# Sliding-window attention with a soft mixture of experts: fp32 scores taken once, two heads side by side, and exponentials transposed on TensorE

## The chip, the core and the metric

The kernel runs on one core of a Trainium2 chip. Five engines work side by side: TensorE (PE; PEld is its weight load), VectorE (DVE), ScalarE (ACT), GpSimd (POOL) and SyncE (SP), which here issues the DMA transfers. Operands lie in SBUF, 128 partitions wide. TensorE writes PSUM, eight banks of 2 KB a partition. The metric is the device time of one execution in microseconds (us).

## What is computed

Attention over 4 batches x 8 heads, 576 positions, 64 wide, with a linear position bias and a causal window of 128; then a soft mixture of 8 experts with 4 slots each; then a two-layer network.

```python
scores = (q @ k.T) / 8                         # (4, 8, 576, 576)
scores = where((rel >= 0) & (rel < 128), scores - slopes * abs(rel), -1e9)   # rel = query - key, slopes = 2**-(h+1)
attn = exp(scores - max(scores)); attn /= sum(attn) + 1e-9
x = (attn @ v)                                 # as (2304, 512)
logits = x @ phi                               # 32 slots
d = softmax of logits over the tokens; slot_input = d.T @ x
slot_out[e] = relu(slot_input[e] @ w1[e]) @ w2[e]
y = softmax of logits over the slots @ slot_out
out = leaky_relu(y @ w_in) @ w_out
```

## The kernel before

The whole program is one stream of units in an order set by numbers. Each unit (a few instructions on one engine) has an offset in a table, `XO` for the 32 heads and `YO` for the router work of the four batches; a head g's unit is due at g plus its offset, the units are sorted by that, and each engine runs its instructions in this order. SyncE's loads are put into the same order: `issue` sends what is due, and between that a few pieces of expert weights (256 KB each, paced by the head's number, as long as there is free SBUF).

For one head the attention goes so:

- Q and K are loaded with two positions in a row of 512 bytes (`load_qk`), and turned by six transposes (L266) into PSUM.
- ScalarE writes the rounded parts `kb`, `qb` (L279, fp32r, the format with which one pass per product is enough), VectorE the rests into `kq` (L284, L286), GpSimd the copies of the rounded parts beside the rests (L292).
- The scores are taken twice. Once with queries on partitions and the rounded parts alone (`smax`, L306): VectorE adds the mask and takes the row maximum (L316). The maxima are transposed (L325), copied (L330) and sent by a DMA (L333) into a row of `qb`, so that the second scores carry them along. Rows of constants in `kb` and `qb` carry the position bias.
- The second time with keys on partitions (`scores`, L351 and L352: rests and rounded parts), 1088 columns in two PSUM tiles. ScalarE takes the exponential of 512 columns at a time (L359), GpSimd sets what lies outside the window to zero (L367 to L377).
- Since keys are on partitions, the exponentials are at once the weights of the products with V (`attend`, L416, 16 products of 65 columns on the two column halves of the array; the 65th column gives the sum).
- VectorE normalizes (L431, L433, L437) into `xs`.

The router work for a batch (`batch_parts`) lies between the heads: transposes of x (L460, L471), logits (L482), maxima over the tokens, slot inputs (L606, L612). Then come the expert products (L839, L891), bound up with the loading of the expert weights, and the network (L1015), 200 us long, with the weights decoded on the way. In the trace, an fp32 product of the program is two instructions (32 for `attend` of a head); a transpose is one.

PSUM in the attention stage: one tile of products with V, `TPB` = 3 tiles "tp" for turns, two "sm" for the first scores, two "st" for the second.

Of the kernel before, what the change touches and what calls it, by code (L numbers as in the profile page):

```python
# [9 lines left out]
F32 = mybir.dt.float32  # L10
F32R = mybir.dt.float32r
# [6 lines left out]
MROW = 96  # L18


@with_exitstack
def attn_softmoe_ffn(ctx: ExitStack, tc: tile.TileContext, q, k, v, phi, w1, w2, w_in, w_out, cst_in, out):
# [12 lines left out]
    TPB = 3  # L35
    R = 3
# [3 lines left out]
    WN = [5, 1, 0, 2, 3, 0, 0]  # L40
    XO = {"Z": -0.1, "TK": -3.1165, "HK": -2.9597, "DK": -2.2105, "LK": -2.68, "TQ": -3.2042, "HQ": -3.0925,
# [4 lines left out]
    YO = {"xt0": 4.4699, "xt0c": 4.6501, "xt1": 5.7337, "xt1c": 5.7794, "xr": 5.5092, "xrc": 5.6877,  # L46
          "lg": 6.5781, "lga": 6.9084, "xt2": 7.4832, "xt2c": 7.6846, "xt3": 9.7716, "xt3c": 9.8712,
          "xs": 9.4718, "xsc": 9.7691, "lh": 10.0639, "lgc": 10.0708, "pm": 10.6372, "lx": 10.7576,
          "bm": 11.6027, "bmv": 11.8446, "ln": 10.8721, "lnc": 10.9955, "bmx": 12.1976, "dxv": 12.0436,
          "dxa": 12.5969, "bt": 12.663, "btv": 12.7744, "bta": 12.9593, "sl": 12.8123, "slv": 13.1223,  # L50
          "ds": 13.3756, "dsv": 13.7379, "tm2": 12.6955, "tme": 13.0753, "cb": 13.9763, "tm3": 12.7455,
          "cb2": 13.9963, "cb3": 14.0163, "cb4": 14.0363}
    ZA = {"DQK": 0.8, "DV": 1.62, "DVS": 1, "W0": -2.2, "EARLY": 0.8, "L0": 3.0, "L1": 4.0,
# [22 lines left out]
    VW = 5 * VH * (D + 1)  # L76
    VP = -(-VW // 16) * 16
    XG = 5 * 4 * D
    sizes = [("nat", 1536), ("ex", 1536 + VP), ("vt1", VP), ("x2", XG), ("vt2", VP), ("vt0", VP), ("pt", 1536), ("x0", XG), ("x1", XG),
# [40 lines left out]
    with tc.manual_schedule():  # L120
# [7 lines left out]
        fctx, cctx = ExitStack(), ExitStack()  # L128
        fr = fctx.enter_context(tc.tile_pool(name="fr", bufs=1, side="right"))
        kb, qb, kq = [], [], []  # L130
        for i in range(R):
            kb.append(fr.tile([128, S], F32R, name=f"kb{i}"))
            qb.append(fr.tile([128, 640], F32R, name=f"qb{i}"))
            kq.append(fr.tile([128, 2 * S + 64], F32R, name=f"kq{i}"))
# [1017 lines left out]
```

## Time and profile before

| What | us |
|---|---|
| Runs of the kernel: median of 3 (lowest to highest) | 435.62 (435.59 to 436.35) |
| Profiled execution: span from first to last instruction | 434.6 |
| TensorE busy / VectorE / ScalarE / GpSimd | 419.8 / 284.1 / 239.0 / 140.5 |
| Attention stage, about | 0 to 165 |
| Expert products, about | 173 to 205 |
| Two-layer network | 205 to 434 |

Of the profiled execution the page gives the span; the times of the runs stand beside it, the median 1.0 us above. How to read it: busy time on TensorE is an upper view, since its products overlap and their ends are modelled; how often instructions start says more. A stage has its own limit, so shares are read by stage. "Idle before" with a name behind an arrow tells who ended a wait.

### The profile page before, as it was taken

The numbers are of one execution on the slowest core, as the hardware profiler recorded it, in microseconds if no ns is written. First come the engines' busy times: TensorE is split into PE (matmuls) and PEld (weight loads), VectorE is DVE, ScalarE is ACT, GpSimd is POOL, SyncE is SP. The second block draws the span as 40 slices with busy tenths as digits, with TensorE's granted clock in tenths as the row PEclk, the third lists the DMA queues.
The fourth block names the chain that finished last, engine by engine and source line by source line (L and its number), as shares of the span: only waits on it lengthen the run. The fifth ranks groups of instructions, "written<-read, shape, count | busy, mean of one in ns | idle before, by whom it ended". The sixth has DMA issues, their size and how long they took to land.

```text
span 434.6 us, 9853 instructions
## 1 busy us (share of the span) xinstructions
PE 419.8 (97%) x3480; PEld 338.2 (78%) x3480; DVE 284.1 (65%) x894; ACT 239.0 (55%) x555; POOL 140.5 (32%) x331
## 2 busy tenths in 40 slices
PE   7898999999999999999999999999999999999996
PEld 6797889888788886333877888788878888888885
DVE  7898899999999964112999885767552233225242
ACT  4586777677678733021886765555554344344440
POOL 6497788687778845020000002020202000000000
PEclk9999999999999999999999999999999999999999
DMA  7768777778867979999987005000000003004012
GB/s 163 222 185 230 227 221 215 219 207 243 229 197 220 261 254 391 321 407 413 411 305 245 31 2 193 2 1 0 2 0 0 2 9 137 0 0 148 0 74 72
DMA packets 66801, 70.15 MB, mean 161 GB/s; under 512 B 23168, under 2 KB 42016, under 8 KB 66752
## 3 DMA queue, kind: packets, MB, share of 16 engines
q1 hardware_dynamic: 66304, 69.24, 49.5%
q8 instruction: 28, 0.46, 0.4%
q10 hardware_dynamic: 448, 0.28, 0.2%
q14 instruction: 21, 0.17, 0.1%
HBM read 64.70 MB, written 4.72 MB: 160 GB/s over the span
## 4 chain that ended last, share of the span: by engine, by line
PE 84%; DVE 6%; DMA 5%; issue 2%; POOL 1%; ACT 1%; DVEq 0%; SPq 0%; POOLq 0%; ACTq 0%
PE acc L1015 45%; PE o_ps L416 6%; PE ph L992 4%; PE sm L306 4%; PE pb L839 3%; PE pb L891 3%; PE st L352 3%; PE st L351 3%; PE tp L266 3%; DMA qb<-ms 2%; DMA ar<-in_q_dram 2%; DVE kq L284 1%; DMA ar<-in_k_dram 1%; PE tp L460 1%; PE tp L482 1%
## 5 line engine op out<-in xcount | busy, mean ns | idle before, releaser
L1015 PE MATMUL acc<-p,p 128*128 128x512 f32 x648 | 158.7, 390 | 0.0
L1015 PEld LDWEIGHTS acc<-p,p 128*128 128x128 f32 x648 | 120.7, 188 | 24.5 <-issue 1.7
L1005 DVE TENSOR_TENSOR p<-ar,p 128x384 fp32r<-128x384 f32 x96 | 52.9, 556 | 89.6 <-ACT ar L1001 89.4
L997 ACT ACTIVATE p<-ph 128x384 fp32r<-128x384 f32 (+1 forms) x97 | 47.5, 491 | 92.4 <-PE ph L992 92.4
L316 DVE CUSTOM_DVE_ANT_0 junk<-sm,ar 128x256 bf16<-128x256 f32 (+2 forms) x160 | 53.6, 374 | 4.5 <-PE sm L306 4.1
L1015 PE MATMUL acc<-b,p 128*128 128x512 f32 x216 | 53.6, 392 | 0.0
L785 POOL TENSOR_TENSOR p<-ar,p 128x512 fp32r<-128x512 f32 x8 | 10.6, 1329 | 124.9 <-ACT p L785 108.7
L359 ACT ACTIVATE ar<-st 128x512 f32<-128x512 f32 x64 | 38.3, 599 | 17.2 <-PE st L352 9.8
L1001 ACT ACTIVATE ar<-ph 128x384 f32<-128x384 f32 x96 | 47.1, 490 | 0.0
L1015 PEld LDWEIGHTS acc<-b,p 128*128 128x128 f32 x216 | 40.1, 188 | 8.2 <-DVE ql L1030 0.4
L416 PE MATMUL o_ps<-ar 128*64 128x65 f32 x992 | 41.3, 227 | 0.0
L416 PEld LDWEIGHTS o_ps<-ar 128*64 128x64 f32 x992 | 36.5, 137 | 4.7 <-issue 1.0
L351 PE MATMUL st<-kq 128*128 128x256 f32 (+1 forms) x160 | 39.7, 277 | 0.0
L352 PE MATMUL st<-qb,kb 128*128 128x256 f32 (+1 forms) x160 | 35.7, 270 | 2.1 <-DMA qb<-ms 2.1
L306 PE MATMUL sm<-kb,qb 128*128 128x256 f32 (+2 forms) x160 | 34.6, 310 | 2.6 <-DVE mn L316 1.0
L279 ACT ACTIVATE qb<-tp 64x288 fp32r<-64x288 f32 x64 | 28.0, 437 | 14.0 <-PE tp L266 13.2
L992 PE MATMUL ph<-p,p 128*128 128x384 f32 x96 | 33.1, 350 | 0.0
L266 PE MATMUL tp<-ident,ar 96*128 96x96 f32 x192 | 28.5, 258 | 2.3 <-DMA ar<-in_q_dram 1.4
L352 PEld LDWEIGHTS st<-qb,kb 128*128 128x128 f32 (+1 forms) x160 | 28.6, 179 | 2.5 <-DMA qb<-ms 2.5
L284 DVE SCALAR_TENSOR_TENSOR kq<-tp,qb 64x288 fp32r<-64x288 f32 x64 | 29.2, 457 | 1.9
L279 ACT ACTIVATE kb<-tp 64x288 fp32r<-64x288 f32 x64 | 28.0, 437 | 4.4 <-PE tp L266 3.0
L286 DVE TENSOR_TENSOR kq<-tp,kb 64x288 fp32r<-64x288 f32 x64 | 29.1, 454 | 1.7
(204 smaller groups left out, 618.0 us busy)
## 6 DMA issues: line engine op xcount, KB each, us to landing
p<-in_moe_w_dram SPq DMA_DIRECT2D x56, 256.0 KB
p<-in_moe_w_dram SPq DMA_DIRECT2D x7, 1024.0 KB
p<-in_moe_w_in_dram SPq DMA_DIRECT2D x5, 1024.0 KB
p<-in_moe_w_out_dram SPq DMA_DIRECT2D x5, 1024.0 KB
ar<-in_q_dram SPq DMA_DIRECT2D x32, 144.0 KB
ar<-in_k_dram SPq DMA_DIRECT2D x31, 144.0 KB
out_dram<-ar SPq DMA_DIRECT2D x17, 256.0 KB
ar<-in_v_dram SPq DMA_DIRECT2D x32, 128.0 KB
```

The source lines that it names most:

```text
L266: nc.tensor.transpose(p[:, 96 * u:96 * u + 96], n[:, 128 * u:128 * u + 128], ident[0:96, 0:96])
L279: nc.scalar.activation(out=b1, in_=pr, func=AF.Copy, scale=2.0 ** (g % H - 2) if half else 1.0)
L306: nc.tensor.matmul(sl, lhsT=Q1[:, 128 * t:128 * t + mr], rhs=K1[:, c0:c1], start=True, stop=True)
L316: nc.vector.tensor_tensor_reduce(out=jk[0:mr, 0:n], in0=sl, in1=maskt[0:mr, m0:m0 + n], op0=ALU.add, op1=ALU.max, accum_out=mn[g % 2][0:mr ...
L351: nc.tensor.matmul(sl, lhsT=KX[:, k0:k1], rhs=QA[:, q0:q1], start=True, stop=False)
L352: nc.tensor.matmul(sl, lhsT=kb[g % R][:, k0:k1], rhs=qb[g % R][:, q0:q1], start=False, stop=True)
L416: nc.tensor.matmul(o_ps[64 * u:64 * u + 64, t, :], lhsT=lt, rhs=r, start=st, stop=sp, tile_position=(0, 64 * u))
L992: nc.tensor.matmul(p, lhsT=mst[:, 128 * f:128 * f + 128], rhs=rhs, start=True, stop=True)
L997: nc.scalar.activation(out=G[t0, f][0][:, c], in_=H1[t0, f][:, c], func=AF.Prelu, alpha=0.01)
L1001: nc.scalar.activation(out=gg, in_=H1.pop((t0, f)), func=AF.Prelu, alpha=0.01)
L1005: nc.vector.tensor_tensor(out=g2, in0=G0.pop((t0, f)), in1=g1.bitcast(F32), op=ALU.subtract)
L1015: nc.tensor.matmul(acc[t0][t], lhsT=(g1, g1, g2)[k][:, 128 * t:128 * t + 128], rhs=(WO1, WO2, WO1)[k][c][:, i], start=(f == f0 and k == 0) ...
```

## The change

Attention works on pairs of heads (i = 0 to 15), and the scores are taken once, in fp32, with queries on partitions.

- Q and K of two heads lie side by side in 128 columns; rows of 64 positions' tiles are loaded in pieces of 256 bytes (`load_qk`, three DMAs for each of Q and K). Positions are cut at 64, 192, 320, 448, so that the first 64 are a tile of their own.
- Eight transposes of 128x128 and two small ones turn them (`turn`, `turn_rest`); head 0 of the pair is then on partitions 0 to 63, head 1 on 64 to 127. One copy on VectorE (K) and one scaled copy on ScalarE (Q) bring them to SBUF, two small ones the rest.
- `scores`: ten fp32 products for a pair, five a head, on 64 rows of the array each, the heads in turn.
- `smax` on VectorE adds mask and position bias (now in the mask tile, loaded as a constant) and writes the sum in fp32 to SBUF beside the maximum. `bias` on GpSimd scales the maxima; `expo` on ScalarE takes the exponential with the maximum as bias, one instruction a block (five a head).
- `flip`: the exponentials are transposed on TensorE, 16 of 128x128 a pair, and copied back to SBUF (`flip_c`, three on ScalarE, one on VectorE).
- `attend`: 17 products a head as before with 64-column weights; each head of the pair has its own PSUM tile.
- Gone: rounded parts and rests, the copies, the transposed maxima and their DMA, the masks and clears on GpSimd.
- All other PSUM tiles of the stage come from one ring of six (`gt`). The tables `XO`, `YO`, `LAST` are new; the router's work is the same, its logits now in two sums for every batch.

```diff
-    XO = {"Z": -0.1, "TK": -3.1165, "HK": -2.9597, ...
+    XO = {"TK": -3.52, "EK": -3.40, "TQ": -3.42, "EQ": -3.31, "TT": -3.32, "ET": -3.2,
+          "S": -2.0, "X0": -1.9, "X1": -1.85, "Y0": -1.7, "Y1": -1.6, ...
...
+        def gt(shape=(128, 512)):
+            return ps.tile(list(shape), F32, tag="g", name="g", bufs=GB)
...
-            put(t.rearrange("p (j c) -> p j c", j=3), src.rearrange("(j p r) d -> p j (r d)", j=3, r=2), n, (half, g))
+            for a in range(2):
+                put(t[:, 0:4, a, :], src[a, 64:S, :].rearrange("(t p) d -> p t d", p=128), n, (half, i))
+            put(t[0:64, 4, :, :], src[:, 0:64, :].rearrange("h p d -> p h d"), n, (half, i))
...
+        def evac_k(i):
+            nc.vector.tensor_copy(kqs[i % R][0][:, 64:S], tps.pop((0, i)))
+
+        def evac_q(i):
+            nc.scalar.activation(out=kqs[i % R][1][:, 64:S], in_=tps.pop((1, i)), func=AF.Copy, scale=qsc[:, i % HB:i % HB + 1])
...
+        BLK = [[(4, 0, 0, 64, 0, 128), (0, 0, 64, 192, 64, 64), (1, 64, 256, 256, 192, 0)],
+               [(2, 192, 0, 256, 320, 0), (3, 320, 256, 256, 448, 0)]]
+
+        def scores(i):
+            K, Q = kqs[i % R]
+            for c in range(2):
+                for a in range(2):
+                    sts[i, a, c] = gt()
+                for t, k0, o, n, q0, m0 in BLK[c]:
+                    for a in range(2):
+                        r = slice(64 * a, 64 * a + 64)
+                        nc.tensor.matmul(sts[i, a, c][:, o:o + n], lhsT=Q[r, q0:q0 + 128], rhs=K[r, k0:k0 + n],
+                                         start=True, stop=True, tile_position=(64 * a, 0))
...
-                        out=jk[0:mr, 0:n], in0=sl, in1=maskt[0:mr, m0:m0 + n], op0=ALU.add, op1=ALU.max,
+                        out=piece(i, a, c)[:, o:o + n], in0=p[:, o:o + n], in1=maskt[:, m0:m0 + n], op0=ALU.add, op1=ALU.max,
...
+        def expo(a, c):
+            def f(i):
+                for t, k0, o, n, q0, m0 in BLK[c]:
+                    e = piece(i, a, c)[:, o:o + n]
+                    j = (t + 1) % 5
+                    nc.scalar.activation(out=e, in_=e, func=AF.Exp, scale=slope(i, a), bias=nb[i % 2][:, a, j:j + 1])
...
+        def flip(a, c):
+            def f(i):
+                pts[i, a, c] = p = gt()
+                e = piece(i, a, c)
+                for j in range(4):
+                    nc.tensor.transpose(p[:, 128 * j:128 * j + 128], e[:, 128 * j:128 * j + 128], ident)
+            return f
+
+        def flip_c(a, c):
+            def f(i):
+                cp = nc.vector.tensor_copy if (a, c) == (0, 1) else nc.scalar.copy
+                cp(out=ptl[2 * a + c], in_=pts.pop((i, a, c)))
```

TensorE in the middle of the stage, before: one head with no router work between (L266 turns, L306 first scores, L351 and L352 second scores, L416 products with V, L325 the transpose of the maxima).

```order
L266 MATMUL tp<-ident,ar 128x96 x3
L306 MATMUL sm<-kb_88,qb_89 128x256 x2
L266 MATMUL tp<-ident,ar 128x96 x3
L416 MATMUL o_ps<-ar 64x65 x16
L325 MATMUL tp<-ident,mn_99 5x128
L306 MATMUL sm<-kb_91,qb_92 64x192
L306 MATMUL sm<-kb_91,qb_92 128x128
L306 MATMUL sm<-kb_91,qb_92 128x256
L351 MATMUL st<-kq_96 128x256
L352 MATMUL st<-qb_95,kb_94 128x256
```

Now, one pair of heads from its second transpose of exponentials on (L331 these transposes of the exponentials, L292 scores, L259 and L265 turns, L354 products with V):

```order
L331 MATMUL g<-ident,ss_90 128x128 x4
L331 MATMUL g<-ident,ss_91 128x128 x4
L331 MATMUL g<-ident,ss_92 128x128 x4
L292 MATMUL g<-kqt 128x64 x2
L292 MATMUL g<-kqt 128x192 x2
L292 MATMUL g<-kqt 128x256 x6
L259 MATMUL g<-ident,ar 128x128 x8
L265 MATMUL g<-ident,ar 128x64 x2
L354 MATMUL o_ps_106<-ar,pt_93 64x65 x9
L354 MATMUL o_ps_106<-ar,pt_94 64x65 x8
L354 MATMUL o_ps_107<-ar,pt_95 64x65 x9
L354 MATMUL o_ps_107<-ar,pt_96 64x65 x8
```

Where a head had its second scores and the products with V with nothing between exponential and product, a pair now has the four transposes of the exponentials (the first stands ahead of these rows), then the next pair's scores, the turns of the pair behind that, and the products with V of the pair whose exponentials were transposed at the start.

VectorE at the same place, before: the rests of Q and K, then a normalization and the maxima of a later head.

```order
L284 SCALAR_TENSOR_TENSOR kq_90<-tp,qb_89 64x288 x2
L286 TENSOR_TENSOR kq_90<-tp,kb_88 64x288 x2
L431 TENSOR_SCALAR rs<-o_ps 128x5
L316 ISA junk,mn_98<-sm,ar 64x192
L316 ISA mn_98 64x1
L433 RECIPROCAL rs<-rs 128x5
L437 TENSOR_TENSOR ar<-o_ps,rs 128x5x64
L316 ISA junk,mn_98<-sm,ar 128x128
L316 ISA mn_98 128x1
L316 ISA junk,mn_98<-sm,ar 128x256
```

Now: the end of a pair's maxima, the copy of K, both normalizations, the copy of one quarter of the transposed exponentials, and the next maxima:

```order
L302 ISA ss_92,mx_99<-g,ar 128x256
L302 ISA mx_99 128x1
L270 COPY kqt<-g 128x512
L366 TENSOR_SCALAR rs<-o_ps_106 128x5
L368 RECIPROCAL rs<-rs 128x5
L373 TENSOR_TENSOR ar<-o_ps_106,rs 128x5x64
L366 TENSOR_SCALAR rs<-o_ps_107 128x5
L368 RECIPROCAL rs<-rs 128x5
L373 TENSOR_TENSOR ar<-o_ps_107,rs 128x5x64
L337 COPY pt_94<-g 128x512
```

The rests are gone; two copies of 128x512 came.

## Rows read from the trace of the kernel before

**Rows 1.** Busy time by stage: stretch, its length, each engine (instructions), clock, DMA share, GB/s.
```profile
60.00:140.00 80.00, 77.28 (x1075) 68.15 (x1074) 76.15 (x320) 58.28 (x143) 62.40 (x155) 1.00 0.77 218
...
170.00:205.00 35.00, 34.82 (x318) 12.69 (x318) 8.00 (x35) 5.63 (x18) 6.05 (x15) 1.00 1.01 381
```

**Rows 2.** VectorE in order of time, one head: start us, us, operation, count.
```profile
90.97 0.17 DVE L431 TENSOR_SCALAR rs<-o_ps 128x5 f32<-128x5 f32 x1
...
92.14 0.42 DVE L316 CUSTOM_DVE_ANT_0 junk<-sm,ar 128x256 bf16<-128x256 f32 x1
...
92.49 0.42 DVE L316 CUSTOM_DVE_ANT_0 junk<-sm,ar 128x256 bf16<-128x256 f32 x1
...
93.29 0.95 DVE L284 SCALAR_TENSOR_TENSOR kq<-tp,qb 64x288 fp32r<-64x288 f32 x2
94.27 0.94 DVE L286 TENSOR_TENSOR kq<-tp,kb 64x288 fp32r<-64x288 f32 x2
95.25 0.17 DVE L431 TENSOR_SCALAR rs<-o_ps 128x5 f32<-128x5 f32 x1
```

**Rows 3.** The chain that ended last, in order of time: start us, us, what.
```profile
9.15 3.19 DMA ar<-in_q_dram
...
22.82 1.19 PE o_ps L416 x32
...
26.41 1.37 PE o_ps L416 x32
...
212.37 2.04 PE acc L1015 x9
```

**Rows 4.** Line 437: duration min/median/max in ns, first and last start.
```profile
L437 DVE TENSOR_TENSOR ar<-o_ps,rs x31: 472/491/493, 25.5 to 164.0; 128x320 f32<-128x320 f32 x31
```

**Rows 5.** TensorE in order of time: start us, us, operation, count.
```profile
90.42 0.60 PE L460 MATMUL tp<-ident,ar 128*128 128x128 f32 x4
...
115.15 1.07 PE L612 MATMUL tp<-ar,dn 128*32 128x256 f32 x16
...
164.19 0.97 PE L416 MATMUL ol<-ar 128*64 128x65 f32 x16 [0.23 <-POOL ar L367]
...
176.21 7.07 PE L839 MATMUL pb<-p,ar 128*32 128x512 f32 x64
```

**Rows 6.** Groups by line and shape up to 190 us: busy us, mean ns, idle before.
```profile
L460 PE MATMUL tp<-ident,ar 128*128 128x128 f32 x64 | 10.2, 279 | 0.0
...
L482 PE MATMUL tp<-ar,phi_sb 128*32 128x144 f32 x128 | 6.0, 293 | 0.3 <-DVE ar L474 0.3
...
L622 DVE COPY SI<-tp 128x512 f32<-128x512 f32 x1 | 0.7, 691 | 0.0
...
L464 ACT COPY ar<-tp 128x256 f32<-128x256 f32 x2 | 0.7, 372 | 2.2 <-PE tp L460 2.2
```

**Rows 7.** The page's groups by line, and those of 173 to 205 us.
```profile
L1015 PE MATMUL acc<-p,p 128*128 128x512 f32 x648 | 158.7, 390 | 0.0
...
L839 PE MATMUL pb<-p,ar 128*32 128x512 f32 x112 | 12.6, 595 | 0.0
```

**Rows 8.** SyncE's queue in order of time.
```profile
1.75 0.42 SPq L158 DMA_DIRECT2D ar<-in_q_dram  x1
...
5.48 3.57 SPq L158 DMA_DIRECT2D ar<-in_v_dram  x6
```

**Rows 9.** Transfers from 6 to 10, 182 to 186 and 60 to 140 us.
```profile
DMA packets 2818, 0.63 MB, mean 157 GB/s; under 512 B 2818, under 2 KB 2818, under 8 KB 2818
...
q1 hardware_dynamic: 2818, 0.63, 76.6%
...
q1 hardware_dynamic: 813, 1.63, 105.1%
...
DMA packets 25559, 17.44 MB, mean 218 GB/s; under 512 B 11203, under 2 KB 20709, under 8 KB 25542
...
q1 hardware_dynamic: 25542, 17.23, 76.1%
```

More of the change, by code (lines that the diff above doesn't have):

```diff
@@ L203, in attn_softmoe_ffn @@
+        for half in (1, 0):
+            load_qk(half, 0)
+        for j in range(3):
+            o, i, _, _ = bulk.pop()
+            nc.scalar.dma_start(out=o, in_=i)
+            send()
+        nc.sync.dma_start(out=maskt, in_=cst_in[:, 0:256])
+        nc.sync.dma_start(out=qsc, in_=cst_in[:, 256:260])
         warm(WN[0])
@@ L233, in attn_softmoe_ffn @@
             load_v(i)
-        issue(0)
+        issue(1)
         pieces = []
@@ L247, in attn_softmoe_ffn @@
         nxt_piece = [0]
-        late = len(pieces) + (off["x0"] - off["vt1"]) // 512 + R * (3 * S + 704) // 512
-        for r, t in pieces[:-3]:
+        late = len(pieces) + (off["x0"] - off["vt1"]) // 512 + 13
+        for r, t in pieces[:-5]:
             queue(r, t)
@@ L312, in smax_v, with turn @@
-        def smax_v(part):
-            def f(g):
-                for t, sl, m0, n, mr in sms.pop((part, g)):
-                    jk = small.tile([128, 256], mybir.dt.bfloat16, tag="junk", name="junk", bufs=2)
+        def turn(half):
+            def f(i):
+                flush((half, i))
+                n = nat(half, i)
+                tps[half, i] = p = gt()
+                for t in range(4):
+                    nc.tensor.transpose(p[:, 128 * t:128 * t + 128], n[:, t].rearrange("p h d -> p (h d)"), ident)
+            return f
@@ new lines, in turn_rest @@
+        def turn_rest(i):
+            tps[2, i] = p = gt()
+            for half in range(2):
+                nc.tensor.transpose(p[:, 64 * half:64 * half + 64], nat(half, i)[0:64, 4].rearrange("p h d -> p (h d)"), ident[0:64, 0:64])
+                if i + 2 < NI:
+                    load_qk(half, i + 2, 2 * i + XO["TT"] + DQK)
+        def evac_k(i):
+            nc.vector.tensor_copy(kqs[i % R][0][:, 64:S], tps.pop((0, i)))
+        def evac_q(i):
+            nc.scalar.activation(out=kqs[i % R][1][:, 64:S], in_=tps.pop((1, i)), func=AF.Copy, scale=qsc[:, i % HB:i % HB + 1])
@@ L478, in f @@
                 def f():
-                    p = ts["lg"] if last and k0 else tp("lg", [128, 144], "sm")
+                    p = ts["lg"] if nm == "li" else tp("lg", [128, 144])
                     for kc in range(k0, k1):
@@ L526, in pm @@
                 m = small.tile([128, 1], F32, tag="pm", name="pm", bufs=1)
-                nc.vector.reduce_max(out=m, in_=ts["lg"] if last else L, axis=AX.X)
+                nc.vector.reduce_max(out=m, in_=L, axis=AX.X)
                 if b == 0:
@@ L657, in attn_softmoe_ffn @@
         for nm, f in UNITS.items():
[L658 to L659 removed]
+            for i in range(NI):
+                ev.append((2 * i + XO[nm], len(ev), lambda f=f, i=i: f(i)))
         for b in range(B):
```

406 lines of the change are left out of this document (141 added, 265 removed), and 8 rows, old and new, of the table XO.

## The prediction

> **What bounds the kernel now.** I read first the table by stage, then the order of time on VectorE and on TensorE, then the transfers. In the attention stage two engines look full: from 60 to 140 us TensorE is busy 77.28 of 80 us and VectorE 76.15, ScalarE 58.28, GpSimd 62.40, the DMA engines 0.77 [rows 1]. Busy time doesn't tell which of the two is the limit, so I took one head on each. On VectorE one head lasts from one L431 to the next, 90.97 to 95.25, 4.28 us, and within it the instructions stand end to end: the casts' rests (L284, L286) in pairs of 0.95 and 0.94, five maxima (L316; a 256-wide one starts 0.35 after the last), and in the 0.6 left one normalization [rows 2]. On TensorE, in the chain of waits, the first products with V of one head start at 22.82 and those of the next at 26.41, 3.59 us, with no router work and no wait between [rows 3]. The mean over the stage is (164.0 - 25.5)/30 = 4.62 us a head, from the first and last start of L437 [rows 4]. So VectorE sets the pace: the 0.34 above its 4.28 are the router's work on it. TensorE needs 32 x 3.59 = 115 us and the router's part (below, 19): 134 after 22.82, so 157, where the last L416 group starts at 164.19 and ends at 165.16 [rows 5]. It is only some 8 us behind VectorE. That is the whole point: a change that relieves VectorE gains at most until TensorE is the limit, and this change also alters what TensorE does. After the stage, 170 to 205 us, TensorE is busy 34.82 of 35 on the expert weights with the DMA engines at 1.01 [rows 1]. The granted clock is 1.00 in all these rows.
>
> **VectorE, ScalarE, GpSimd: what goes and what comes, for a pair of heads.** The casts' rests go (2 x 1.9 us), and the masks, copies and clears on GpSimd; four small bias products stay there. VectorE keeps ten maxima (64, 192 and three times 256 wide for each head; at 0.35 or less 3.5 us), keeps two normalizations (1.2), and gets two copies of 128x512 out of PSUM, which the trace has once, at 0.69 [rows 6]: 6.1, with the router's 0.7 about 6.8, where it was 9.2. The maxima now write fp32 instead of bf16; I count this at nothing, and if it cost 0.1 us each VectorE would be at 7.8. ScalarE gets ten exponentials of at most 256 columns for two of 512, at 0.37 for a 256-column copy [rows 6] at most 3.7, four passes over 128x512 at no more than VectorE's 0.69 and two small ones, 3.2: 6.9, and about 1 for the router. Both stay under what follows for TensorE, which hides them.
>
> **TensorE, for a pair.** The prices are steps from start to start, since its intervals overlap: the length of a group less one duration, over the number of steps.
> - Transposes: four in 0.60 with 0.279 each is (0.60 - 0.28)/3 = 0.107 [rows 5, 6]; I take 0.115 for the changes between groups. The exponentials are 16 of them, 1.85 us, all new. K and Q take 10 instead of 12, 1.15.
> - Scores. Gone are the rounded scores and the two-term scores with the transpose of the maxima. New are ten fp32 products, each on 64 rows, 1024 columns a head. A 512-column pass is 2.04/9 = 0.227 us on L1015 [rows 3]. An fp32 product shows in the trace as two instructions, each of 595 ns at 512 columns against the 390 of L1015, so of two passes [rows 7]: 1024 x 4 passes x 0.227/512 = 1.8 us a head. If the two heads, which stand on different halves of the array's rows and write different banks, run at the same time, that is 1.8 a pair; if one after the other, 3.6. The trace has no product on half the rows. The nearest row is L839: 64 fp32 instructions on four column quarters in 7.07 us [rows 5], 0.10 each, where one alone would need 0.45. I take the overlapped end, nearest to this row, and 0.2 for entering and leaving: 2.0. Both ends stay for the range.
> - Products with V: 34 for 32, in two runs instead of four. A head's run takes 1.19 to 1.37 [rows 3]: 2.6.
> - The router's part is kept. Four L460 groups of 0.45, two L482 groups (16 of 128, 0.75 each by their busy time), L612 with 1.07 [rows 5, 6], and by these prices some 1.5 of smaller ones: 5.8 a batch, 1.4 a pair.
>
> Sum: 1.85 + 1.15 + 2.0 + 2.6 + 1.4 = 9.0 us a pair, where the pace now is 9.24. TensorE's own work doesn't fall; it rises a little (7.6 against 7.2 without the router). What is won is the difference to VectorE's pace, and the start.
>
> The Trainium skill puts a figure on the product on half the rows, "TensorE: Matmul & The Clock Gate", Part 3: four row tiles came to 3.07 times the speed of one after the other, 77% of four. Two tiles at 77% would make 2.3 us of the 1.8, and 7 us on the whole sum; no run here shows it yet.
>
> **The start.** The third head's Q comes behind V on SP; the chain waits for this transfer from 9.15 on, for 3.19 us [rows 3]. In the changed order eleven SP loads (three for each of Q of pair 0, Q and K of pair 1, and two constants) stand ahead of V, twelve of V, the router's matrix, and then six for pair 2. At 0.45 for the first kind (0.42 for one of Q) and 0.6 for V (six in 3.57) [rows 8] that is, from 0.8 on, 5 + 7.7 + 2.6, so 16.1; with 3 us to land 19. The turns of pair 2 stand in TensorE's row ahead of the products of pair 0, so these start at about 19, two heads at once, where the first head's start at 22.82 now. From 17 to 22 is possible.
>
> **The sum.** From 19 on: 16 runs of 2.6 (41.6), 15 times the exponentials (27.8), 14 scores (28), 13 turns (15), the router less its tail (19): 131. TensorE stood idle 3.4% of the time in [rows 1], 2.72 of 80; with as much, 136. The stage ends at 155 instead of 165.2: 10 us. The tail has one addition more on VectorE, 0.3 us. Everything behind it is as before. 434.6 - 10 + 0.3 = 425 us of span; the median of the runs is 1.0 above the span, so about 426, and I say 425.5.
>
> **Transfers.** Q and K now come in rows of 256 bytes, twice as many packets. From 6 to 10 us all 2818 packets were under 512 bytes and took 76.6% of 16 engines: 17.4 ns each [rows 9]. A packet of the weights takes 1.051 x 64 / 813 = 83 ns [rows 9]. From 60 to 140 us, 76.1% of 1280 engine-us less 11203 x 17.4 and 4833 x 83 ns leaves 378 for 9506 packets of 512 bytes: 40 ns [rows 9]. So two short ones cost 35 where a long one cost 40; nothing is lost. The Trainium skill, "DMA: Bandwidth & Descriptors", Specifications, speaks against the change: line rate needs 512 bytes or more. By that rule a short packet would cost what the long one does and the stage's 0.77 would become over 1.0, which is the second rival; the row at 17.4 ns disagrees. On SP a pair issues 10 loads of Q, K and V and as many weights as before, for 7 loads and two of the maxima; at 0.45 these 14 or 15 issues take 6.5 us of 9, as now. Weights are paced by heads, so as many lie in SBUF at the stage's end.
>
> **The rivals.**
> First, slower: the two heads' score products run one after the other. Each pair then costs 1.6 to 1.8 us more on TensorE, in 14 of 16 pairs (two lie in the start): +25, so 450. It decides from 0.7 us a pair on, where the 10 us are used up; so more than half the overlap has to be there. For it: no row has a product on half the rows. Against it: the four quarters of L839, and the loops issue the two heads in turn. 0.13.
> Second, the transfers become the limit. By the rule above Q and K would cost 18432 x 40 ns / 16 = 46 us more of the DMA engines; 0.77 x 155 + 46 = 165 us, the stage would end where it does now: 434 to 437. A milder form is that the weights, at 1.01 behind the stage, come a few us late. The rows speak against the full form. 0.10.
> Third, TensorE waits in its order. From the start of a pair's scores to its last exponential lie 1.2 (first tiles), up to 3.5 of maxima, and the bias and the last two exponentials, about 1: 5.7 us; TensorE fills 5.75 ahead of the first transpose of exponentials and 7.1 ahead of the last. This fits with 1 us to spare; the six PSUM tiles that all now share could take it away. Each us a pair costs 14: 432 to 440. 0.14.
> Fourth, better than the sum: fewer waits than 3.4%, or an earlier start: 411 to 417. 0.08.
>
> **How the numbers follow.** The forecast, 417 to 431, has 0.55. The second and third rivals lie on both sides of the time before; about a third of each is within 0.2%, which is about what a measurement of this kernel can tell from no change. Faster 0.71, same 0.08, slower 0.21. The range 415 to 442 leaves out the first rival (0.13) and a little at the lower end.
>
> **What would show it.** Right: VectorE under 75% busy from 60 to 140 us and TensorE as full as now; the last normalization near 156; start-to-start of the two heads' score instructions far below their duration, a pair's scores in about 2 us; transposes at 0.11; short packets still at 17 to 18 ns. Wrong: a pair's scores in 3.6 us, TensorE waiting on ScalarE ahead of the transposes of the exponentials, the first products with V later than 22 us, or waits on DMA in the weights' stage.

## The result and the profile after

The changed kernel takes **440.57 us** (median of six runs, 439.27 to 442.10), the kernel before 435.75 (six runs beside them). The ratio is 1.010, with a 95% interval of 1.007 to 1.013: slower by about 1%. 425.5 was predicted; the time lies in the range of 415 to 442, but on the other side of the kernel before. The profiled execution has a span of 439.9 us, and its time is 441.92. All comparisons here are between undisturbed runs, except where a granted clock below 1.00 is named with the row.

The same two stretches as in [rows 1], with the same columns:

```profile
60.00:140.00 80.00, 76.06 (x1100) 64.02 (x1097) 56.92 (x272) 56.46 (x154) 8.25 (x36) 1.00 0.87 223
170.00:205.00 35.00, 33.32 (x303) 13.75 (x303) 10.95 (x48) 6.40 (x20) 7.36 (x19) 1.00 0.87 325
```

VectorE fell from 76.15 to 56.92 us and GpSimd from 62.40 to 8.25, as the change meant; TensorE is nearly as full as it was, 76.06 where it had 77.28. The relief was real, and the kernel is slower all the same.

Where the loss lies, three rows tell: the products with V and the normalization (first and last start, answering [rows 4]), and the matmuls of the last stage from the page (answering [rows 7]):

```profile
L354 PE MATMUL o_ps<-ar,pt x1088: 218/222/272, 26.9 to 169.9; 128*64 128x65 f32 x182
...
L373 DVE TENSOR_TENSOR ar<-o_ps,rs x33: 292/492/493, 28.6 to 170.8; 128x320 f32<-128x320 f32 x31, 128x128 f32<-128x128 f32 x1, 128x192 f32<-128x192 f32 x1
...
L945 PE MATMUL acc<-p,p 128*128 128x512 f32 x648 | 158.7, 390 | 0.0
```

The last product with V starts at 169.9; before it was at 164.9:

```profile
L416 PE MATMUL o_ps<-ar x992: 220/222/272, 22.8 to 163.3; 128*64 128x65 f32 x199
L416 PE MATMUL ol<-ar x32: 220/222/272, 163.2 to 164.9; 128*64 128x65 f32 x32
```

From there to the end of the span lie 439.9 - 169.9 = 270.0 us after and 434.6 - 164.9 = 269.7 before. The same 270 us, within 0.4, end every run below, so what follows needs two numbers only: the **first** product with V (the start) and the **way** from the first to the last (the steady part). Before: 22.8 and 142.1. Forecast: 19 and 136. After: 26.9 and 143.0. So 7.9 us of the miss lie in the start and 7 in the steady part.

**The start**, from the chain of waits (start us, us, what); it answers the first lines of [rows 3]:

```profile
2.19 3.48 DMA ar<-in_k_dram
...
5.80 1.09 PE g L259 x4
6.89 0.85 PE g L157 x4
...
11.00 3.93 PE g L292 x20
...
20.94 2.04 PE g L292 x20
...
26.97 1.19 PE o_ps L354 x34
```

K lands at 5.67, and then no transfer is waited for: TensorE itself is the path. Two things stand in it. L157 are filler products (two between any two pieces of the start, printed as four since an fp32 product is two instructions); those between the pieces take 25.5% of the view's 32 us, 8.2 us. And TensorE works at half speed: the first score group of 20 takes 3.93 us where the next takes 2.04, the first turn of K 1.09 where it takes 0.63 at full speed (below). This is the lower of the two levels of TensorE's clock, 1.2 GHz. A row for these us prints 1.00 only because the trace holds no record of the clock before 15.0 us, where the upper level, 2.4 GHz, begins; the durations change at the same place. TensorE had stood from 3.9 to 5.8 us, waiting for K.

**The steady part.** The row of the whole way (columns as in [rows 1]), TensorE's waits from 20 to 165 us (us in total, times, longest), and a pair in the chain that ended last, in order of time:

```profile
26.90:169.90 143.00, 134.98 (x2038) 114.84 (x2038) 96.88 (x451) 99.60 (x270) 13.73 (x60) 1.00 0.89 239
```

```profile
PE g L417 <- ACT ar L409: 5.8, 4, 1.4
PE g L292 <- ACT pt L337: 1.2, 3, 0.4
```

```profile
60.84 0.24 POOL nb L313
...
61.10 2.08 ACT ss L321 x6
63.18 0.57 ACT kqt L273
63.75 0.80 ACT ss L321 x2
...
64.86 0.80 ACT ss L321 x2
65.65 0.47 ACT ar L399
66.12 0.17 ACT ar L409
...
66.33 0.70 PE g L417 x16
67.03 1.90 PE g L331 x16
68.93 1.23 PE g L292 x12
```

TensorE is busy 135.0 of the 143.0 us and idle 8.0, where the forecast had 131 and 5. The idle part is told by the waits and the chain: bias, ten exponentials (with copies of Q between them), two copies for the router, then the router's logits (L417) and only behind them the transposes of the exponentials (L331). The logits product stands ahead of the transposes in TensorE's order and waits for a copy that stands behind all exponentials in ScalarE's. So from the first exponential to the last copy, 5.2 us, ScalarE is the chain. TensorE's own work of that time, the products with V, ends at 64.9, and it stands until 66.3.

### The profile page after: what moved, and what is told of

Its sections match the earlier page's. It is cut to its first block, busy times and chain, and to the rows that moved or that the text cites. A ratio compares the mean times of both kernels' runs of the same rounds, so it can differ in the third digit from the quotient of the medians.

```text
span 439.9 us, 9567 instructions
## 1 busy us (share of the span) xinstructions
PE 422.9 (96%) x3584; PEld 335.8 (76%) x3584; DVE 244.7 (56%) x790; ACT 238.5 (54%) x587; POOL 34.7 (8%) x103
## 4 chain that ended last, share of the span: by engine, by line
PE 86%; ACT 7%; DVE 3%; issue 1%; DMA 1%; POOL 0%; ACTq 0%; DVEq 0%; POOLq 0%
PE acc L945 45%; PE g L292 7%; PE g L331 6%; PE o_ps L354 5%; ACT ss L321 5%; PE ph L922 4%; PE pb L769 3%; PE pb L821 3%; PE g L259 2%; PE g L157 2%; PE g L417 1%; PE g L395 1%; DVE ss L302 1%; PE g L544 1%; PE ph L872 1%
## 5 line engine op out<-in xcount | busy, mean ns | idle before, releaser
L945 PEld LDWEIGHTS acc<-p,p 128*128 128x128 f32 x648 | 120.7, 188 | 24.5 <-issue 1.7
L321 ACT ACTIVATE ss<-ss,nb 128x256 f32<-128x256 f32 (+2 forms) x160 | 62.0, 456 | 30.3 <-POOL nb L313 30.3
L302 DVE CUSTOM_DVE_ANT_0 ss<-g,ar 128x256 f32<-128x256 f32 (+2 forms) x160 | 48.0, 367 | 22.2 <-PE g L292 22.1
L292 PE MATMUL g<-kqt 64*128 64x256 f32 (+2 forms) x320 | 37.0, 370 | 1.2 <-ACT pt L337 1.2
L354 PE MATMUL o_ps<-ar,pt 128*64 128x65 f32 x1088 | 37.2, 225 | 0.0
L354 PEld LDWEIGHTS o_ps<-ar,pt 128*64 128x64 f32 x1088 | 34.9, 137 | 2.1 <-issue 1.6
L337 ACT COPY pt<-g 128x512 f32<-128x512 f32 x48 | 26.1, 589 | 14.0 <-PE g L331 13.6
L292 PEld LDWEIGHTS g<-kqt 64*128 64x128 f32 x320 | 28.1, 195 | 6.1 <-issue 2.7
L331 PE MATMUL g<-ident,ss 128*128 128x128 f32 x256 | 31.4, 275 | 0.0
L331 PEld LDWEIGHTS g<-ident,ss 128*128 128x128 f32 x256 | 28.1, 141 | 1.6 <-issue 1.4
L715 DVE SCALAR_TENSOR_TENSOR ar<-ar 128x512 int32<-128x512 int32 x40 | 25.7, 686 | 0.2
L313 POOL TENSOR_SCALAR nb<-mx 128x3 f32<-128x3 f32 (+1 forms) x64 | 14.3, 224 | 130.5 <-DVE mx L302 127.0
L259 PE MATMUL g<-ident,ar 128*128 128x128 f32 x128 | 18.8, 288 | 1.9 <-DMA ar<-in_k_dram 1.9
```

The source lines that it names most:

```text
L259: nc.tensor.transpose(p[:, 128 * t:128 * t + 128], n[:, t].rearrange("p h d -> p (h d)"), ident)
L292: nc.tensor.matmul(sts[i, a, c][:, o:o + n], lhsT=Q[r, q0:q0 + 128], rhs=K[r, k0:k0 + n], start=True, stop=True, tile_position=(64 * a, 0))
L302: nc.vector.tensor_tensor_reduce(out=piece(i, a, c)[:, o:o + n], in0=p[:, o:o + n], in1=maskt[:, m0:m0 + n], op0=ALU.add, op1=ALU.max, acc ...
L321: nc.scalar.activation(out=e, in_=e, func=AF.Exp, scale=slope(i, a), bias=nb[i % 2][:, a, j:j + 1])
L331: nc.tensor.transpose(p[:, 128 * j:128 * j + 128], e[:, 128 * j:128 * j + 128], ident)
L354: nc.tensor.matmul(o[64 * u:64 * u + 64, t, :], lhsT=p[:, x:x + 64], rhs=V[:, w, a, :], start=st, stop=sp, tile_position=(0, 64 * u))
```

## The experiments

**Is the loss in the start and in the order?** Three edits of the changed kernel, one each: more warm-up products ahead of K's landing, no filler products, the logits later in TensorE's order.

```diff
-    WN = [5, 2, 0, 2, 3, 0, 0]
+    WN = [10, 2, 0, 2, 3, 0, 0]
```


> The changed kernel with ten instead of five idle products on TensorE ahead of the first transposes, which cover its wait for K from 3.9 to 5.8 us. Theory (start): after this wait TensorE works at half speed until about 15 us (first scores 4.0 us instead of 2.11, transposes 0.27 apart instead of 0.11), and every step of the start stands on that; the first products with V come at 22 to 24 us instead of 26.9 and the whole is 3 to 5 us faster, 436 to 437.5. Rival: the start waits for loads (SP issues the third pair's Q until 19.1 us), and the first products come no earlier than 26: no change beyond 1 us.

```diff
-    WN = [5, 2, 0, 2, 3, 0, 0]
+    WN = [5, 0, 0, 2, 3, 0, 0]
```


> The changed kernel without the 26 filler products that TensorE runs between the pieces of the start (13 pairs of products). Theory: they lie on the path from the landing of K at 5.7 to the first products with V; without them TensorE gets there until the transfer of the third pair's Q, which lands at 21 to 22, holds it: first products with V at 22.5 to 24 instead of 26.9, time 436 to 438. Rival: TensorE's speed falls without them and the first products come no earlier than 25: 439 to 441.

```diff
-          "lg": 5.44, "lga": 5.6, ... "lh": 9.44, "lgc": 9.55, "pm": 9.7, "lx": 9.65,
+          "lg": 5.95, "lga": 6.05, ... "lh": 9.95, "lgc": 10.05, "pm": 10.06, "lx": 10.07,
```


> The changed kernel with the router's logit products (line 417) moved from just ahead of a pair's transposes of the exponentials to just behind them, with what follows from them. Theory (waits in order): TensorE stood for some 1.4 us at these products in 4 places, for a copy that ScalarE has queued behind the exponentials, though the transposes behind it were ready; 5 to 6 us faster, about 435. Rival: the transposes wait for the same exponentials, the wait only moves to the next instruction: within 1 us of 440.6.

| kernel | first product | last | way | median us | ratio to before (95%) |
|---|---|---|---|---|---|
| changed | 26.9 | 169.9 | 143.0 | 440.57 | 1.010 (1.007 to 1.013) |
| longer warm-up | 23.7 | 167.1 | 143.4 | 439.12 | 1.0074 (1.0047 to 1.0101) |
| no fillers | 22.5 | 165.6 | 143.1 | 437.45 | 1.0043 (1.0021 to 1.0064) |
| logits later | 24.5 | 164.4 | 139.9 | 436.12 | 1.0013 (0.998 to 1.0047) |

First products and ways move as the theories said; the time of the longer warm-up, 439.12, stays above the 436 to 437.5 that was expected. The fillers cost 4.4 us of start, compared at the same half speed of the first scores (then Q of the third pair holds: its transfer ends at 20.7). With the longer warm-up the first turn takes 0.63 and the first scores 2.04, from its chain:

```profile
5.73 0.63 PE g L259 x4
...
8.59 2.04 PE g L292 x20
```

The logits are worth 3.1 us of the way; the 2.4 of start in that row belong to the start itself, which differs from one execution to the next: the trace's clock record begins at 9.7 us there and at 15.0 in the changed kernel's, so that its first scores already run at full speed. Against a start like that the longer warm-up is worth 0.8 us, against the changed kernel's 3.2. The waits with the logits later show what comes next:

```profile
PE g L259 <- DMA ar<-in_k_dram: 2.5, 3, 1.2
PE g L259 <- DMA ar<-in_q_dram: 1.9, 5, 0.5
...
PE g L417 <- ACT ar L409: 0.7, 1, 0.7
```

**What the overlap of the two heads is worth, and whether TensorE is the limit after.** The score loops in another order: inside each tile one head first, then (second edit) a whole head first; and one more transpose in each group of the exponentials.

```diff
-                for t, k0, o, n, q0, m0 in BLK[c]:
-                    for a in range(2):
+                for a in range(2):
+                    for t, k0, o, n, q0, m0 in BLK[c]:
```


> The changed kernel, with the score products of one head issued one after another and then those of the other, instead of in turn; the same products and results. If the two heads' products run at the same time in the changed kernel (20 instructions in 2.11 us), this takes the overlap away: a pair's scores should take 3.5 to 3.8 us and the time rise by 14 pairs x 1.6 = 22 us, to about 462. If the overlap does not depend on the order, or was never there, the time stays at 440.

```diff
-            for c in range(2):
-                ...
-                for t, k0, o, n, q0, m0 in BLK[c]:
-                    for a in range(2):
+            for a in range(2):
+                for c in range(2):
+                    for t, k0, o, n, q0, m0 in BLK[c]:
```


> The changed kernel with all ten fp32 score instructions of one head ahead of those of the other (before: the two heads in turn). Theory: the two heads overlap on the array only where their instructions stand next to each other; a pair's scores then take 3.2 to 3.6 us instead of 2.04, 1.2 to 1.5 more in 14 pairs, of which TensorE's waits can take up about 0.4: 451 to 457. Rival: the pace is set elsewhere than on TensorE, and the scores' length does not matter: 441 to 444.

```diff
-                for j in range(4):
+                for j in (0, 1, 2, 3, 0):
```


> The changed kernel with one transpose of each four done twice, four more 128x128 transposes a pair, 64 in all, with the same result. If TensorE is the limit through the whole stage, each costs its step of 0.11 us: 7 us slower, 447 to 448. If TensorE waits for the exponentials in each pair (a chain through VectorE, GpSimd and ScalarE sets the pace), less than half of that shows: under 444.

Measured: 441.08 (ratio 1.0101, 1.004 to 1.0162; way 144.2), 448.74 (1.028, 1.0246 to 1.0313; way 149.9), 445.23 (1.0196, 1.0135 to 1.0258; way 148.3). A pair's scores in the chains of the first and the second:

```profile
67.39 2.31 PE g L292 x19
```

```profile
71.30 3.13 PE g L293 x19
```

So with the two heads in turn 20 instructions take 2.04 us, in blocks of two or three 19 of them take 2.31, a whole head at a time 3.13: the overlap exists, and it needs neighbours in TensorE's order. (Three pairs of 14 take 2.9, in turn and in blocks alike; in turn the group waits 0.4 us in its middle there for a copy out of PSUM, the second row of TensorE's waits above.) My first expectation for the blocks, 462, was wrong because blocks of two or three still overlap; the second, 451 to 457, was too high too. By rows like that of the whole way above, TensorE's busy time rose from 135.0 to 147.4 us with a whole head at a time, and its idle time fell from 8.0 to 2.6; the difference, 6.9, is what reached the way. Of the 7 us of extra transposes 5.3 did. TensorE is the limit of the changed kernel for the larger part of the stage, and the rest is its waits.

**Was VectorE the limit before?** On this the forecast rested. Five edits of the kernel before. One rest of the casts left out on VectorE (the second scores then lack its term; zeros stand there), and both:

```diff
+            nc.gpsimd.memset(kq[i].bitcast(F32)[0:64, 0:S], 0.0)
...
-                    else:
-                        nc.vector.tensor_tensor(out=x2, in0=pr, in1=b1.bitcast(F32), op=ALU.subtract)
```


> The kernel before without one of the two rests of the casts on VectorE (the K rest, about 0.95 us a head; the second scores then lack the term with that rest). Theory: VectorE sets the pace of the attention stage before; with 3.33 + 0.34 us a head it would fall behind TensorE's 3.59 and its router work, so the stage follows TensorE and the kernel ends 5 to 8 us earlier: 428 to 431. Rival: TensorE or the transfers already set the pace, VectorE is full beside it: 434 to 436.

```diff
             def low_(g):
-                for pr, b1, x2 in pieces(g):
-                ...
+                pass
```


> The kernel before without either rest of the casts on VectorE (about 1.9 of its 4.28 us a head; the second scores then lack the terms with the rests). VectorE has nothing left that could set a pace of 4.6 us. Theory (formed after the run that left out one rest): TensorE, with the round trip of the maxima through DMA, set the pace of the attention stage before, and VectorE was only full beside it: 433 to 436. Rival, the prediction's own premise: VectorE set the pace, and the stage now follows TensorE: 426 to 430.

One transpose more per group of Q and K:

```diff
-                for u in range(3):
+                for u in (0, 1, 2, 0):
```


> The kernel before with one 96x96 transpose more in each of the 64 groups of Q and K (the first is done twice), 64 x 0.10 = 6.4 us more on TensorE, nothing on VectorE. Theory: TensorE sets the pace before, so most of it comes through: 441 to 443. Rival, the prediction's premise: TensorE has 8 us to spare behind VectorE, and 2 us or less come through: 436 to 438.

The round trip of the maxima left out, alone and with both rests; and the round trip on another queue:

```diff
         def mtr_d(g):
-            nc.sync.dma_start(out=qb[g % R][MROW:MROW + 1, :]...
+            mss.pop(g)
```


> The kernel before without the transfer that carries the rounded maxima back into the second scores (17 of it between 60 and 140 us, one a head; the second scores then lack the maxima). From the first to the last product with V lie 142.1 us in the kernel before, 142.7 without the rests, 142.7 with more transposes. Theory: this transfer, in order on SP behind the wait for the maxima, closes the loop that sets the pace; without it 135 to 138 us from the first to the last product, time 429 to 432. Rival one, VectorE after all: nothing changes as long as the rests are there: 435 to 437. Rival two, TensorE: the same 435 to 437, and the next kernel tells which.

> The kernel before without that transfer and without the rests of the casts (the second scores lack both). Theory: VectorE and the round trip are two limits of nearly the same length, each of which holds the pace when the other is taken away; without both 132 to 136 us from the first to the last product with V, time 428 to 432 (a first product as late as 27 as without the rests alone would add 4). Rival: TensorE itself sets the pace: 141 to 143 us, time 436 to 440.

```diff
-            nc.sync.dma_start(out=qb[g % R][MROW:MROW + 1, :]...
+            nc.scalar.dma_start(out=qb[g % R][MROW:MROW + 1, :]...
```


> The kernel before with the transfer of the maxima issued on ScalarE's queue, right behind the copy that makes them, instead of on SP's. If it is SP's order that makes the round trip long, the stage gets shorter by 2 to 5 us: 431 to 434. If it is the landing of the transfer itself (about 2 us), or another limit: 435 to 437; and slower, 438 to 440, if 0.7 us of issue a head on ScalarE holds its casts.

| kernel before, with | first product | last | way | median us | ratio (95%) |
|---|---|---|---|---|---|
| nothing changed | 22.8 | 164.9 | 142.1 | 435.75 | |
| one rest out | | | | 437.08 | 0.9996 (0.9964 to 1.0028) |
| both rests out | 27.3 | 170.0 | 142.7 | 439.20 | 1.0057 (1.0032 to 1.0082) |
| transposes added | 23.1 | 165.8 | 142.7 | 438.19 | 1.0022 (0.9994 to 1.005) |
| round trip out | 23.1 | 162.7 | 139.6 | 434.17 | 0.992 (0.9889 to 0.9951) |
| both rests and round trip out | 27.0 | 161.8 | 134.8 | 433.70 | 0.9898 (0.9831 to 0.9966) |
| round trip on ScalarE's queue | | | | 441.93 | 1.0098 (1.0063 to 1.0132) |

(Two rows have no way: their profiled executions had a granted clock of 0.96 from 60 to 100 us.) VectorE relieved of 1.9 us a head: the way does not move. TensorE loaded with 6.4 us: it does not move either. What does hold it then is read from TensorE's waits; first rows, in this order, of both rests out and of the round trip out:

```profile
PE st L350 <- DMA qb<-ms: 5.7, 6, 1.9
```

```profile
PE tp L325 <- DVE kq L284: 1.2, 4, 0.5
PE sm L306 <- DVE mn L316: 0.9, 2, 0.5
```

Without the rests it is the transfer of the maxima; without the transfer it is VectorE. Without both, the row from 60 to 100 us is TensorE end to end:

```profile
60.00:100.00 40.00, 39.81 (x571) 36.13 (x570) 25.63 (x133) 30.60 (x75) 33.42 (x82) 1.00 0.85 229
```

and the way is 134.8 us. So **two limits of nearly the same length** (139.6 and 142.7) stood in front of TensorE's own 134.8, each holding the pace when the other is taken away. This is shown.

Is it the transfer's landing or its issue in SP's order? On ScalarE's queue the kernel is slower by 1%, which doesn't tell them apart, since 0.70 us of issue a head then stands among ScalarE's casts. The chain without the rests does: from the start of its issue to its landing the transfer takes 4.15 us in the row below, and the issue is 0.72 of that. The landing is the larger part.

```profile
59.99 0.10 PE st L350
60.09 4.15 DMA qb<-ms
...
64.29 0.38 PE st L350
```

In the two kernels without both rests the first product comes 4 us later, which is why their times say less than their ways. This is the edit's own doing: the zeros that stand for the rests are written by VectorE at the start, from 5.4 to 9.7 us, ahead of a row of constants that the first scores need. TensorE's wait for it, without the rests:

```profile
PE sm L304 <- DVE kb L224: 4.7, 1, 4.7
```

**Does the changed kernel beat both when mended?** Four edits at once (ten warm-up products, one filler for two, logits later, and eight loads of V on ScalarE's queue):

```diff
-    WN = [5, 2, 0, 2, 3, 0, 0]
+    WN = [10, 1, 0, 2, 3, 0, 0]
...
+        for j in range(8):
+            o, i, _, _ = bulk.pop(0)
+            nc.scalar.dma_start(out=o, in_=i)
```


> The changed kernel with four things at once: ten first warm-up products instead of five, one filler product instead of two between the pieces of the start, the eight loads of V of the second and third pair on ScalarE's queue, and the logits products later in TensorE's order. Theory: the start and the waits on the logits are what the change lost; first products with V at 19 to 20.5, from there to the last ones 140 to 141 us, time 429 to 433, faster than both kernels. Rival: what the start gains comes back as waits on the transfers of Q and K later: 434 to 437.

435.05 us, ratio **0.9963** (0.9944 to 0.9982): faster than both, by 0.4% and some 1.3%, though not the 429 to 433 expected. First product at 24.7, way 137.8. The start did not get shorter: its chain runs through the V loads in ScalarE's queue. Behind them stand the load of ScalarE's function table (the 1.28 us) and the copies of Q.

```profile
4.08 4.20 DMA ar<-in_v_dram
...
8.30 0.61 ACTq L230
...
9.66 1.28 ACT L276
```

So next no filler at all, V of the third pair on SP behind its Q and K, ten warm-ups and the later logits; run twice, since its first profile had a granted clock of 0.93 from 60 to 100 us:

```diff
-    WN = [5, 2, 0, 2, 3, 0, 0]
+    WN = [10, 0, 0, 2, 3, 0, 0]
...
-        for i in range(1, NVB):
+        for i in range(1, NVB - 1):
             load_v(i)
...
+            if i == 0:
+                load_v(NVB - 1, XO["TT"] + DQK)
```


> The changed kernel with ten first warm-up products, no filler products between the pieces of the start, the loads of the third pair's Q and K ahead of those of its V on SP, and the logits products later in TensorE's order. Theory: first products with V at 19 to 20.5, as the prediction had them, and from there 139 to 141 us as in the run with four edits (24.7 to 162.5 there): 430 to 432.5. Rival: the loads that come earlier at the start are missing later, TensorE waits for Q and K, and no more than 1 us is won over the run with four edits: 434 to 435.

> The same kernel as the one with the short start (ten first warm-up products, no filler products, the third pair's Q and K ahead of its V, logits later), since the profiled execution of that one had a granted clock of 0.93 from 60 to 100 us and so cannot tell where the 4 us that the start won were lost. Theory: at a granted clock of 1.00 from the first to the last product with V lie 140 to 142 us, and the time is 433 to 434 in such an execution. Rival: SP's issue of the loads holds TensorE, 143 to 145 us at full clock too.

Ratios 0.9975 (0.9951 to 1.000) and 0.9966 (0.9932 to 1.000), medians 436.01 and 435.20: no better than the four edits, and above what was expected of either. The first product comes at 20.7 and 20.2, nearly the 19 of the forecast, but the way is 145.8 and 144.3. In the first, TensorE's clock has a part. TensorE waited for a transfer of K from 56.1 to 57.7 us, and from 58.8 to 65.6 the lower level was granted, which is worth some 3.4 us at half speed (the row of 60 to 100 us):

```profile
60.00:100.00 40.00, 39.47 (x542) 33.60 (x541) 25.50 (x120) 26.29 (x71) 3.25 (x14) 0.93 0.88 223
```

In the second the clock is 1.00 there, and TensorE waits:

```profile
PE g L259 <- ACT ss L323: 3.5, 5, 1.3
PE g L259 <- DMA ar<-in_k_dram: 2.9, 5, 0.9
PE g L259 <- DMA ar<-in_q_dram: 1.9, 6, 0.5
```

What the start wins the way gives back. Is it SP's issue of loads? All V loads on GpSimd's queue, in the kernel with the later logits, in the one with the short start, and there with the bias products on VectorE too:

```diff
-            nc.sync.dma_start(out=o, in_=i)
+            (nc.gpsimd if key[0] == "v" else nc.sync).dma_start(out=o, in_=i)
...
-                nc.gpsimd.tensor_scalar(out=nb[i % 2][:, a, r], ...
+                nc.vector.tensor_scalar(out=nb[i % 2][:, a, r], ...
```


> The changed kernel with the logits products later and all loads of V issued on GpSimd's queue instead of SP's. SP's issues fill some 71 of 80 us in the changed kernel (32 of V at 0.605, 27 of K at 0.507, 27 of Q at 0.594, 38 of weights at about 0.5). Theory: with the logits' wait gone, SP's issues hold TensorE (waits on Q and K of 4.4 us there); without V on SP the last product with V comes 3 to 5 us earlier than 164.4: 431 to 433. Rival: the landing, not the issue, is late, or TensorE's own work is the limit: 435 to 437; slower, 438 to 442, if GpSimd's issues hold the small products of the bias that ScalarE's exponentials wait for.

> The kernel with the short start, and all loads of V issued on GpSimd's queue. Theory: the short start (first products with V at 20) is then not given back, since SP keeps up: last product with V at 157 to 160, time 427 to 431. Rival: ScalarE's exponentials or the landing of Q and K hold the pace as in the run with the short start (144.3 us from first to last product): 434 to 437.

> The kernel of the run before this one (short start, all V on GpSimd's queue), with the small products of the bias on VectorE, so that no exponential waits for GpSimd any more (16 waits, 50.9 us in the run before). Theory: SP's issues were what gave the shorter start back; first products with V at 19.5 to 21, the last at 157 to 160, time 427 to 431. Rival: ScalarE's exponentials and TensorE's order hold the pace, and the last products come at 162 to 165 again: 434 to 437.

460.37, 450.82 and 444.63 us: all slower, by 1.8 to 5%. They don't answer the question, since each makes a new wait in GpSimd's order: first (of the second kernel) the exponentials for the bias, which stands behind loads that wait for their buffer, then (third kernel) the router for a product on GpSimd. Behind such waits the clock fell as well: it was at the lower level from 14.9 to 28.6 us in the second kernel, TensorE having stood from 11.7 on, and from 70.6 to 80.8 in the third, where TensorE stood from 67.1 to 75.4.

```profile
ACT ss L323 <- POOL nb L315: 50.9, 16, 14.3
```

```profile
PE g L452 <- POOL ar L447: 8.3, 1, 8.3
```

Whether SP's issues or ScalarE's exponentials hold the mended kernel **stays open**.

## Why the prediction was wrong

**The prices on TensorE held for a pair, the sum did not.** Per pair: transposes of the exponentials 1.90 (1.85 said), scores 2.04 to 2.11 (2.0), turns 1.02 + 0.27 (1.15), products with V 2.24 (2.6). Together 7.5 where 7.6 was said, and the first rival fell. The Trainium skill has 3.07 times for four row tiles ("TensorE: Matmul & The Clock Gate", Part 3); an estimate from that, 77% for two tiles, would have made the scores 2.3 us; the 2.04 here are 88% of the ideal 1.8. But the sum of 131 came out as 135.0 busy (the row of the way). Added up from start to start without the idle gaps, the router's products take 23 us of it where the sum had 19 and where the same products took 19 in the kernel before; the scores 30 for 28, the turns 17 for 15, the products with V 36 for 42. Why the router's products are dearer in the new order was not tried; short waits hidden under modelled ends may be in it.

**"It is only some 8 us behind VectorE": half right.** TensorE's own 134 us after the first product are confirmed by 134.8 with nothing in front of it. But VectorE was not the only thing in front; the round trip of the maxima was as long, and I had not read it as a limit, though the waits and SP's queue of the kernel before have it (TensorE's longest wait from 28 to 160 us, and 0.72 us of issue a head):

```profile
PE st L352 <- DMA qb<-ms: 2.1, 2, 1.3
```

```profile
L333 SPq DMA_DIRECT2D qb<-ms x17: 708/717/757, 60.3 to 137.4; - x17
```

The relief of VectorE alone was worth nothing. That it did no harm to the forecast is luck: the change removes the round trip too.

**The start failed: "these start at about 19".** I summed SP's loads and nothing else. TensorE's own row in the start, with 8.2 us of fillers and the first groups at half speed, ends later than the loads: 26.9, and 24.5 to 25.2 in three other executions with the same warm-up and fillers, where the clock rose earlier. Without fillers it was 22.5, with a longer warm-up as well and the loads in another order 20.2 to 20.7.

**The waits failed: "with as much, 136".** I carried the idle share of the old order, 3.4%, over to the new one, where it is 8.0 of 143.0 us, 5.6%. The third rival named the right thing, with too small a price and the wrong chance (0.14). It said 5.7 us from a pair's scores to its last exponential, with 1 us to spare. In the chain above it is 7.2 (the scores start at 58.4, the last exponential ends at 65.7), because the path is another: I had it run along VectorE's ten maxima with two exponentials behind them. It runs along ScalarE, which starts at 61.1 and needs 4.6 from the first to the last exponential. The ten together take 3.7, as I had said (two of 256 columns in 0.80, though each lasts 0.50 by the group's mean below, since they overlap); the rest are copies of the next Q and K between them. The group of 256 columns (busy us, mean ns, idle before):

```profile
L321 ACT ACTIVATE ss<-ss,nb 128x256 f32<-128x256 f32 x49 | 22.8, 499 | 0.0
```

The router's copies follow, and its logits product stands in the way. Moving that gave 3.1 us back.

**Transfers: wrong size, no consequence.** From 60 to 140 us:

```profile
DMA packets 36017, 17.85 MB, mean 223 GB/s; under 512 B 31018, under 2 KB 31018, under 8 KB 36003
...
q1 hardware_dynamic: 36003, 17.67, 86.1%
```

1102 engine-us, less 4985 packets of weights at 83 ns, leave 22.2 ns for a short packet. Two cost 44 where I said 35 and a long one cost 40: a little is lost, not nothing. The Trainium skill ("DMA: Bandwidth & Descriptors", Specifications) wants 512 bytes or more for line rate. My reading of it for the second rival, that a short packet costs what a long one does, the 22.2 ns don't bear out. TensorE waited for no transfer from 20 to 165 us, so the second rival fell as well. SP's issue was mis-sized more:

```profile
L163 SPq DMA_DIRECT2D ar<-in_v_dram x32: 378/605/1540, 64.6 to 134.5; - x32
L163 SPq DMA_DIRECT2D ar<-in_k_dram x27: 378/507/1576, 60.8 to 137.8; - x27
L163 SPq DMA_DIRECT2D ar<-in_q_dram x27: 505/594/1194, 62.4 to 139.7; - x27
```

0.51 to 0.61 where I took 0.45. With 38 weights at about 0.47 these are 67 of 80 us at the medians, not 6.5 of 9.

**VectorE, ScalarE's load, and all behind the stage held**: VectorE is at 71% (under 75% was said) and ScalarE also at 71%, and the 270 us after the last product are unchanged.

In sum: 15 us later than forecast at the stage's end, 7.9 by the start and 7 in the way, of which by this row some 4 are TensorE's own work and 3 idle time in order. Of the 6 us that were expected in the way (142.1 to 136) the kernel with four edits has 4.3 (137.8); of the 4 in the start (22.8 to 19) the short start has 2.6 (20.2). No run has both, and the best time is 0.4% below the kernel before.

## What to carry to other kernels

An engine that is full without a gap need not be the limit: look for a second chain of the same length, and take each away alone and then both before a gain is booked on either. What stands in for the work left out must not cost time of its own: here zeros written at the start cost 4 us. When a change writes a stage anew, sum TensorE's own row in the start, with every warm-up and filler product, beside the loads; and for every product that waits for another engine ask what stands behind it in the queue. Idle time of the old order says nothing of the new one, and a product's price in the old order need not hold in the new one.

## What the runs showed of the hardware

- TensorE began each execution of the changed kernel and its edits at the lower level of its clock, 1.2 GHz: the first warm-up products start some 230 ns apart, later ones 112. With five warm-up products and 1.7 to 2.2 us of idle time behind them the upper level came at 9.0 to 15.0 us (seven executions), with ten and work almost to the landing of K at 4.4 to 7.6 (six). A row for the time before prints 1.00, since the traces have no record there; the durations tell (a turn in 1.09 for 0.63, scores in 3.93 for 2.04).
- Products on half the rows overlap with those on the other half only near each other in the order: 2.04 us for 20 instructions in turn; for 19 of them 2.31 in blocks of two or three, 3.13 a head at a time.
- One execution of the short start was granted a clock of 0.93 from 60 to 100 us, with TensorE busy 39.47 of 40 us: the lower level from 58.8 to 65.6, behind a wait for K from 56.1 to 57.7. Another of the same kernel had 1.00 there, with TensorE busy 37.80 and no wait over 1 us between 50 and 60. How long a wait it takes was not tried.
- A load of V took 0.70 to 0.78 us to issue on GpSimd's queue, 0.605 on SP's; and a load that waits for its buffer holds every small product behind it (16 waits of ScalarE for the bias, 50.9 us, the longest 14.3).
